# Output projection in four parts with a two-term fold, projections in half passes, and another order of the segment's units

## The chip, the cores and the metric

The kernel runs on one core of a Trainium2 chip. The metric is the device time of one execution in microseconds (us). The unchanged kernel took 1058.44 us (median of 3 runs, 1056.85 to 1059.75). The profiled execution, from which every other time in this part comes, took 1050.84 us; its span from the first to the last instruction is 1049.0 us.

## What is computed

There are two attention branches over the same input and a gate between them. Branch A is a recurrence: 64 segments of 32 rows, and each segment needs the memory that the segment before it produced. Branch B has no such chain over segments of 32; it is work that can be put anywhere.

```python
# A: x (1, 2048, 512); mem (8 rows, 512); Wq, Wk, Wv (512, 32 heads, 128); Wo (32, 128, 512)
for s in range(64):
    h = concat([mem, x[:, 32*s:32*s+32]])                 # 40 rows
    q, k, v = h @ Wq, h @ Wk, h @ Wv                      # per head
    p = softmax(where(mask, q @ k.T * 128**-0.5, -1e9))
    o = sum over heads of (p @ v) @ Wo                    # 40 rows of 512
    mem = o[:, :8]; outs.append(o[:, 8:])                 # a
# B: causal attention in 4 blocks of 512 rows, 32 heads of 16, plus a linear memory; then @ wo   # b
g = sigmoid((x * gate_w).sum(-1, keepdims=True))
return g * a + (1 - g) * b
```

## The kernel before

**Phases.** A first phase loads x and B's weights, transposes x, makes B's projections and stores them in DRAM, while A's weights (four of 4 MB) arrive. From about 86 us on, 64 segments follow (`segment`, called by `plan_a`), each some 14 to 17 us long. A short end follows.

**The recurrence.** `hT[s % 2]` holds a segment's first 32 columns, transposed: 8 of memory and 24 rows of x. These 32 columns are handled alone. The last 8 rows of each segment do not depend on the memory until their queries meet the keys, so the keys, queries and values of the last 8 rows of four segments are projected together, ahead of time, by `left_units`; their output rows are projected together by `ol_units`, a group of four segments later.

**A segment's units.** Each engine executes its own instructions in the order in which they were recorded, and the order of recording is the string `A_ORDER` (line 823), walked once per segment. Its units are:

- `Q0 Q1 K0 K1 V0 V1` (`nat_pass`): a projection pass, 16 heads at a time. `proj` (line 855, matmuls at L862) issues 16 matmuls of 512 columns: four contraction chunks `c` and four column groups `j` of the array, which run side by side. Then comes an eviction of the PSUM bank (`evac`, L319 on ScalarE, L321 on VectorE).
- `TK`, `TQ` (`tr`): 32 x 32 block transposes on VectorE (L868).
- `S` (`scores`, L1006 to L1013, and the exponential at L1019), `M` (`sums`, L1036, then a logarithm L1040 and exponential L1043 which give the reciprocal), `N` (`norm`, L1047 for the main and L1051 for the left part, both on VectorE).
- `PV` (`pv`, L1061 and L1070), and `E0a` to `E1b`: the evictions of its four banks in two halves to `OT_sb`.
- `W0`, `W1` (`wo`, through `out_rows`, matmul at L899): the output projection. For each of 32 heads, each of the four column groups `j` computes its own 128 output columns of that head, so there are 128 matmuls of 128 columns with 128 weight loads. The result (32 rows in each of the four groups) is evicted by ScalarE to `aW_sb`.
- `WT` (`w_t`): one VectorE transpose writes the memory columns of the next segment's `hT`, and GpSimd copies the 24 output rows on to `aT_st`.
- Fillers: `Fc` takes the next `left_units` or `ol_units` pass, `Ff` the next light unit (a gating tail: `brow` at L949, `atr` at L964), `bS` and `bP` a score and a value block of B (L706 with its exponential L714, and L753), `bT` a late piece of B. In three segments of four the two `Fc` are left passes; in the fourth (segments 3, 7, 11 ...) they are the two halves of the previous group's output rows, 64 matmuls each.

`A_ENG` (line 826) says which engine makes each eviction. PSUM has eight banks of 512 f32 columns; `Banks` hands them out while the program is recorded, so a matmul that reuses a bank waits for the eviction that emptied it, whichever unit that belongs to. GpSimd's operations each wait for the one before.

Of the kernel before, what the change touches and what calls it, by code (L numbers as in the profile page):

```python
# [223 lines left out]
def build(nc, es, A_x, A_mem0, A_Wq, A_Wk, A_Wv, A_Wo, B_wq, B_wk, B_wv, B_wo, B_beta, gate_w, out, dbg=None):  # L224
    v = NS()
# [30 lines left out]
    def alloc(stack, *specs):  # L256
        for name, shape, dt, n in specs:
# [3 lines left out]
    alloc(es, ("ident", [128, 128], BF16, 0), ("xT", [128, C, S], BF16, 0), ("hT", [128, C, 128], BF16, 2),  # L261
# [9 lines left out]
          ("aTg", [128, C, 128], BF16, 0))  # L271
# [13 lines left out]
          ("OT_sb", [128, H, L], BF16, 0), ("OTL", [128, H, SEG], BF16, 2), ("aW_sb", [128, 128], BF16, 0), ("aO_sb", [128, 128], BF16, 0),  # L285
# [16 lines left out]
    def Rs(name):  # L302
        if name not in R:
            R[name] = Res(name)
            if name.startswith(("P0", "P1", "Pn", "R0", "R1", "OT", "aW", "aO", "t1", "aTx", "aTl")):
                R[name].readers = list(v.stores)
        return R[name]
# [60 lines left out]
def plan_const(v):  # L368
# [28 lines left out]
    def late():  # L397
        rob, rmk = Rs("onesb"), Rs("mneg")
        gp(lambda g: g.memset(onesb[:], 0.0), rob, "onesb0", True)
        gp(lambda g: g.memset(mneg[:], 0.0), rmk, "mneg0", True)  # L400
        for j in range(4):
# [88 lines left out]
def plan_gates(v):  # L490
# [27 lines left out]
    v.evac("dve", v.hT[0][:, :, 0:v.M], v.pb16[bk][:, 0:C * v.M].rearrange("p (c t) -> p c t", t=v.M), [bk], [Rs("hTm0")], "memT0")  # L518
# [119 lines left out]
class BAttn:  # L638
# [167 lines left out]
    def finish(self, sb, f):  # L806
# [3 lines left out]
        def ft(pe):  # L810
            ins = None
            for q in range(4):
# [11 lines left out]
    Q1 K0 Q0 K1 V0 TK0 TQ0 S0 bP bP TQ1 TK1 bS V1 M0 S1 N0 Fc M1 PV0 E0a N1 E0b Fc PV1 E1b E1a W0 W1 WT bS bT Ff Ff Ff  # L824
    bS bP bS""".split()
A_ENG = dict(K0="act", K1="act", Q0="act", Q1="dve", V0="act", V1="dve", KL0="dve", KL1="dve", QL0="dve", QL1="dve", VL0="dve",
             VL1="dve", OL="act", W="act", E0a="act", E0b="act", E1a="act", E1b="act", last=0)


def plan_a(v, nseg):  # L830
# [10 lines left out]
    OT_sb, OTL, aW_sb, aO_sb, t1_sb, aT_st, g_sb, omg_sb, out2d, g_out = (  # L841
        v.OT_sb, v.OTL, v.aW_sb, v.aO_sb, v.t1_sb, v.aT_st, v.g_sb, v.omg_sb, v.out2d, v.g_out)
# [12 lines left out]
    def proj(bk, lhs, w_sb, b, split, reads, name):  # L855

        def f(pe):
            ins = None
            for c in range(C):
# [33 lines left out]
    def out_rows(bk, b, lhs, reads, name):  # L893

        def f(pe):
            ins = None
            for h in range(16 * b, 16 * (b + 1)):
                for j in range(4):
                    ins = pe.matmul(pb[bk][SEG * j:SEG * (j + 1), 0:128], lhs(h), cols(Wo_sb[:, h, :], j), start=(h == 0), stop=(h == H - 1))  # L899
            return ins  # L900
        P.op("pe", f, reads=reads + [Rs("Wo")], writes=[rbank[bk]], name=name)

    def ol_units(g):
# [5 lines left out]
        for b in range(2):  # L909
            def u(b=b):  # L910
                if b == 0:
                    st["bk"] = B.take(long=True)
                bk = st["bk"]
                out_rows(bk, b, lambda h: OTL[par][:, h, :], [Rs("OTL%d" % par)], "ol%d_%d" % (g, b))
                if b == 1:
                    evac(ENG["OL"], aO_sb[:, :], pb[bk][:, 0:128], [bk], [Rs("aO")], "olev%d" % g)
                    B.give(bk)
            units.append(("c", u))

        def ut():  # L920
            flip(aT_st[par][:, :, :].rearrange("p c (r t) -> p c r t", t=SEG)[:, :, :, SEG - 8:SEG],
                 aO_sb[:, :].rearrange("p (c r i) -> p c r i", c=C, i=8), [Rs("aO")], [Rs("aTl%d" % par)], "aTl%d" % g)
# [55 lines left out]
    def segment(s, fill):  # L978
# [3 lines left out]
        rx = [Rs("hTx%d" % (s % 2)), Rs("hTm%d" % (s % 2))]  # L982

        def nat_pass(m, b, eng):
            w_sb, wr, nat = {"K": (Wk_sb, "Wk", KN_sb), "Q": (Wq_sb, "Wq", QN_sb), "V": (Wv_sb, "Wv", V_sb)}[m]
            bk = B.take()
            proj(bk, lhs, w_sb, b, m != "V", rx + [Rs(wr)], "%s%d_%d" % (m, s, b))
# [11 lines left out]
        def scores(b):  # L999
            bk = sbk[b] = B.take()  # L1000

            def f_sc(pe):
# [8 lines left out]
                for i in range(4):  # L1011
# [6 lines left out]
                 writes=[rbank[bk]], name="sc%d_%d" % (s, b))  # L1018
# [205 lines left out]
```

## Time and profile before

| of the profiled execution | |
|---|---|
| span | 1049.0 us |
| TensorE matmuls busy | 910.7 us (87%) in 30127 |
| weight loads | 562.9 us (54%) in 30149 |
| VectorE busy | 558.5 us (53%) |
| ScalarE busy | 585.8 us (56%) |
| GpSimd busy | 228.1 us (22%) |
| granted TensorE clock | 0.974 |
| segment 30, the third of its four (first projection matmul at 536.6 us, the next segment's at 550.9) | 14.3 us |
| segment 31, the fourth of its four (550.9 to 568.0) | 17.1 us |

The page's groups of instructions name a line, an engine, an operation, its tiles and shape, then the count, the busy time, the mean duration of one in ns, and the idle time of the engine just before them with what ended it. "issue" as the end of an idle time means that the engine waited for nothing that the profile shows. The chain of waits follows the program back from its last instruction, at each step to what released it. The row for DMA queue q8 counts the blocks of instructions themselves that were fetched while the program ran.

### The profile page before, as it was taken

The numbers are of one execution on the slowest core, as the hardware profiler recorded it, in microseconds if no ns is written. First come the engines' busy times: TensorE is split into PE (matmuls) and PEld (weight loads), VectorE is DVE, ScalarE is ACT, GpSimd is POOL, SyncE is SP. The second block draws the span as 40 slices with busy tenths as digits, with TensorE's granted clock in tenths as the row PEclk, the third lists the DMA queues.
The fourth block names the chain that finished last, engine by engine and source line by source line (L and its number), as shares of the span: only waits on it lengthen the run. The fifth ranks groups of instructions, "written<-read, shape, count | busy, mean of one in ns | idle before, by whom it ended". The sixth has DMA issues, their size and how long they took to land.

```text
span 1049.0 us, 65298 instructions
## 1 busy us (share of the span) xinstructions
PE 910.7 (87%) x30127; PEld 562.9 (54%) x30149; DVE 558.5 (53%) x1198; ACT 585.8 (56%) x1211; POOL 228.1 (22%) x603
## 2 busy tenths in 40 slices
PE   7967999789898989899898989989898889988786
PEld 4434565555555555555555555655556555555555
DVE  4665545454454646455465646545564655546433
ACT  4442665565565655655565556655665665554434
POOL 6100221122221222222222222222222222211010
PEclk9997999999999999999999999999999999999989
DMA  9896000000101110010001101000111101000110
GB/s 310 271 373 187 12 12 17 13 21 12 26 15 29 46 37 23 15 25 20 21 16 50 40 15 35 20 23 14 24 46 27 28 20 37 14 14 4 40 33 10
DMA packets 65929, 52.23 MB, mean 50 GB/s; under 512 B 34288, under 2 KB 64120, under 8 KB 64120
## 3 DMA queue, kind: packets, MB, share of 16 engines
q1 hardware_dynamic: 65656, 48.06, 15.6%
q8 instruction: 236, 3.87, 1.5%
q14 instruction: 37, 0.30, 0.1%
HBM read 33.47 MB, written 14.57 MB: 46 GB/s over the span
## 4 chain that ended last, share of the span: by engine, by line
PE 73%; issue 9%; ACT 8%; DVE 6%; DMA 3%; POOL 0%; SPq 0%; ACTq 0%; POOLq 0%; DVEq 0%
PE ps L862 33%; PE ps L899 17%; PE ps L706 5%; ACT PT L714 4%; PE ps L753 4%; PE ps L582 2%; PE ps L557 2%; DVE LN_sb L321 2%; PE ps L1061 2%; ACT R_sb L1043 2%; ACT R_sb L1040 2%; DVE Pn_sb L1047 2%; PE ps L949 1%; DMA Wo_sb<-in_A_Wo_dram 1%; DVE VL L321 1%
## 5 line engine op out<-in xcount | busy, mean ns | idle before, releaser
L899 PE MATMUL ps<-Wo_sb,OT_sb 128*32 128x128 bf16 x8192 | 150.8, 228 | 58.2 <-issue 54.3
L714 ACT ACTIVATE PT<-ps 128x1024 bf16<-128x1024 f32 x160 | 160.1, 1023 | 25.5 <-PE ps L706 21.2
L899 PEld LDWEIGHTS ps<-Wo_sb,OT_sb 128*32 128x32 bf16 x8192 | 126.3, 101 | 72.9 <-issue 62.2
L722 POOL TENSOR_SCALAR_AFFINE_SELECT PT<-PT 128x256 bf16<-128x256 bf16 (+1 forms) x224 | 98.4, 439 | 268.3 <-ACT PT L714 261.0
L862 PE MATMUL ps<-Wq_sb,hT 128*32 128x512 bf16 x2048 | 139.3, 388 | 2.5 <-DVE hT L868 1.9
L868 DVE STREAM_TRANSPOSE hT<-aW_sb 128x128 bf16<-128x128 bf16 x64 | 19.9, 311 | 222.1 <-ACT aW_sb L319 222.1
L862 PE MATMUL ps<-Wk_sb,hT 128*32 128x512 bf16 x2048 | 137.6, 385 | 0.3 <-issue 0.3
L862 PE MATMUL ps<-Wv_sb,hT 128*32 128x512 bf16 x2048 | 134.4, 380 | 0.8 <-ACT V_sb L319 0.8
L319 ACT ACTIVATE KN_sb<-ps 128x512 bf16<-128x512 f32 x128 | 76.4, 597 | 101.1 <-PE ps L862 79.1
L319 ACT ACTIVATE OT_sb<-ps 128x320 bf16<-128x320 f32 x256 | 96.9, 430 | 54.2 <-PE ps L1070 53.2
L868 DVE STREAM_TRANSPOSE KT_sb<-KN_sb 128x512 bf16<-128x512 bf16 x128 | 88.3, 690 | 45.6 <-ACT KN_sb L319 45.3
L319 ACT ACTIVATE aW_sb<-ps 128x128 bf16<-128x128 f32 x64 | 17.8, 278 | 153.8 <-PE ps L899 150.3
L868 DVE STREAM_TRANSPOSE QT_sb<-QN_sb 128x512 bf16<-128x512 bf16 x128 | 83.5, 690 | 10.5 <-ACT QN_sb L319 9.8
L862 PEld LDWEIGHTS ps<-Wk_sb,hT 128*32 128x32 bf16 x2048 | 57.6, 99 | 57.6 <-issue 4.8
L1129 POOL COPY OTL<-OT_sb 128x256 bf16<-128x256 bf16 x64 | 25.4, 397 | 289.8 <-ACT OT_sb L319 289.8
L321 DVE CAST V_sb<-ps 128x512 bf16<-128x512 f32 x64 | 44.3, 692 | 74.7 <-PE ps L862 74.7
L862 PEld LDWEIGHTS ps<-Wq_sb,hT 128*32 128x32 bf16 x2048 | 51.5, 98 | 58.9 <-issue 11.6
L862 PEld LDWEIGHTS ps<-Wv_sb,hT 128*32 128x32 bf16 x2048 | 50.5, 96 | 54.1 <-ACT P_sb L1019 9.8
L321 DVE CAST QN_sb<-ps 128x512 bf16<-128x512 f32 x64 | 43.9, 685 | 39.4 <-PE ps L862 39.1
L706 PE MATMUL ps<-QTj,KTj 32*128 32x384 bf16 (+3 forms) x512 | 63.7, 307 | 0.0
L1047 DVE TENSOR_TENSOR Pn_sb<-P_sb,R_sb 128x160 bf16<-128x160 bf16 x128 | 42.5, 332 | 30.0 <-ACT R_sb L1043 20.7
L1040 ACT ACTIVATE R_sb<-ps 128x160 f32<-128x160 f32 x128 | 38.9, 304 | 34.8 <-PE ps L1036 34.5
(117 smaller groups left out, 1412.5 us busy)
## 6 DMA issues: line engine op xcount, KB each, us to landing
Wk_sb<-in_A_Wk_dram SPq DMA_DIRECT2D x4, 1024.0 KB, 5.9
Wq_sb<-in_A_Wq_dram SPq DMA_DIRECT2D x4, 1024.0 KB, 7.3
Wv_sb<-in_A_Wv_dram SPq DMA_DIRECT2D x4, 1024.0 KB, 9.2
Wo_sb<-in_A_Wo_dram SPq DMA_DIRECT2D x4, 1024.0 KB, 10.7
scr_vd<-V SPq DMA_DIRECT2D x16, 136.0 KB, 6.0
Vj<-scr_vd SPq DMA_DIRECT2D x32, 68.0 KB, 2.4
Wo_sb<-in_A_x_dram SPq DMA_DIRECT2D x4, 512.0 KB, 7.5
scr_kTd<-stgk SPq DMA_DIRECT2D x16, 128.0 KB, 7.1
```

The lines of the kernel that those rows point to most:

```text
L319: P.op("act", lambda a: a.activation(dst, src, ACT.Copy), reads=[v.rbank[k] for k in bks], writes=dres, name=name)
L321: P.op("dve", lambda d: d.tensor_copy(dst, src), reads=[v.rbank[k] for k in bks], writes=dres, name=name)
L706: ins = pe.matmul(v.pb[bks[x]][:, o:o + w], KT[e][r, 128 * kc:128 * (kc + 1)], QT[r, q0:q0 + w], start=True, stop=True, tile_position=(r.s ...
L714: P.op("act", lambda a: a.activation(pt[:, :, :], v.ps[:, bks[0]:bks[1] + 1, :], ACT.Exp, scale=v.SCALE_B), reads=[v.rbank[b] for b in bks ...
L722: P.op("gp", lambda g, mv=mv: g.affine_select(mv, mv, [[0, mv.shape[1]], [1, 128]], ALU.is_ge, 0.0, base=0, channel_multiplier=-1), reads= ...
L753: ins = pe.matmul(v.pb[ob][:, o:o + 17], pt[:, x, col:col + 128], V[:, kc, 17 * h:17 * (h + 1)], start=first, stop=True, skip_group_check= ...
L862: ins = pe.matmul(pb[bk][SEG * j:SEG * (j + 1), :], lhs(c), cols(w, j) if split else w[:, 512 * j:512 * (j + 1)], start=(c == 0), stop=(c ...
L868: P.op("dve", lambda d: d.transpose(dst, src), reads=reads, writes=writes, name=name)
L899: ins = pe.matmul(pb[bk][SEG * j:SEG * (j + 1), 0:128], lhs(h), cols(Wo_sb[:, h, :], j), start=(h == 0), stop=(h == H - 1))
L1040: P.op("act", lambda a: a.activation(R_sb[:, b, :], pb[bk][:, 224:384], ACT.Ln), reads=[rbank[bk]], writes=[Rs("R%d" % b)], name="ln%d_%d" ...
L1047: P.op("dve", lambda d: d.tensor_tensor(wide(Pn_sb, b)[:, :, 0:L], wide(P_sb, b)[:, :, 0:L], R_sb[:, b, :].rearrange("p (i q) -> p i q", q ...
L1129: P.op("gp", lambda gq: gq.tensor_copy(OTL[par][:, :, 8 * r:8 * r + 8], OT_sb[:, :, SEG:L]), reads=[Rs("OT%d_%d" % (c, hf)) for c in range ...
```

## The change

**Output projection.** `out_rows` becomes `out_part`. Column group `j` now takes heads 4k + j instead of a quarter of the columns, and a matmul covers 256 output columns in one of two banks (`hf`), so there are 64 matmuls of 256 columns. Each group then holds a partial sum over 8 heads, and the four must be added. `part_hi` (ScalarE) copies the partial sums to bf16 (`WH`), `part_lo` (VectorE) stores what that rounding lost (`WL`), and `fold` multiplies both by a 0/1 matrix, which adds the four groups and transposes the result at once: 8 matmuls of 32 columns. The memory goes from there straight to the next `hT`, the other rows straight to `aT_st`, all on VectorE. The transpose on VectorE and GpSimd's copy are gone. `ol_units` is changed in the same way, with `LN_sb` as its buffer.

**Half passes.** `hT`'s memory columns are now two pieces of dependence (`hTm0_0`, `hTm0_1`), and each projection pass is two units, `x` (chunks 0, 1) and `y` (chunks 2, 3), so that a pass may begin when half of the memory is there. Evictions, exponentials and reciprocals are units of their own (`k q v X L n H l`).

**Order and engines.** A new `A_ORDER` and `A_ENG`: the left passes' evictions go from VectorE to ScalarE, `E0a` goes from ScalarE to VectorE, the left part of the normalisation from VectorE to GpSimd, and late pieces of B (`bT`) come in the middle of the output projection instead of after it.

```diff
 A_ORDER = """
-    Q1 K0 Q0 K1 V0 TK0 TQ0 S0 bP bP TQ1 TK1 bS V1 M0 S1 N0 Fc M1 PV0 E0a N1 E0b Fc PV1 E1b E1a W0 W1 WT bS bT Ff Ff Ff
-    bS bP bS""".split()
-A_ENG = dict(K0="act", K1="act", Q0="act", Q1="dve", V0="act", V1="dve", KL0="dve", KL1="dve", QL0="dve", QL1="dve", VL0="dve",
-             VL1="dve", OL="act", W="act", E0a="act", E0b="act", E1a="act", E1b="act", last=0)
+    Q1x Q1y K0x K0y Q0x Q0y k0 K1x K1y V0x q0 q1 V0y k1 TK0 TQ0 v0 S0 TQ1 bP X0 bS V1x TK1 V1y M0 L0 v1
+    S1 N0 X1 Fc M1 L1 n0 n1 PV0 E0a E0b N1 Fc bP PV1 W0a E1b W0b E1a bT W1b W1a H0 H1 bP l0 l1 bS
+    Ff F0 F1 hm0 hm1 Ff bS ax Ff""".split()
+A_ENG = dict(K0="act", K1="act", Q0="act", Q1="dve", V0="act", V1="dve", KL0="act", KL1="act", QL0="act", QL1="act", VL0="act", VL1="act", OL="act", ax="dve", hm="dve", n="gp", E0a="dve", E0b="act", E1a="act", E1b="act", last=0)
...
-            for c in range(C):
+            for c in cs:
...
-    def out_rows(bk, b, lhs, reads, name):
+    def out_part(bks, hf, ks, first, lhs, reads, name):
 
         def f(pe):
             ins = None
-            for h in range(16 * b, 16 * (b + 1)):
+            for k in ks:
                 for j in range(4):
-                    ins = pe.matmul(pb[bk][SEG * j:SEG * (j + 1), 0:128], lhs(h), cols(Wo_sb[:, h, :], j), start=(h == 0), stop=(h == H - 1))
+                    ins = pe.matmul(pb[bks[hf]][SEG * j:SEG * (j + 1), 0:HD], lhs(4 * k + j), Wo_sb[:, 4 * k + j, HD * hf:HD * (hf + 1)],
+                                    start=(first and k == ks[0]), stop=False, skip_group_check=True)
             return ins
...
+    def part_hi(bks, hf, hi, res, name):
+        c = slice(HD * hf, HD * (hf + 1))
+        P.op("act", lambda a: a.activation(hi[:, c], pb[bks[hf]][:, 0:HD], ACT.Copy), reads=[rbank[bks[hf]]],
+             writes=[Rs(res[0][hf])], name="%sh%d" % (name, hf))
+
+    def part_lo(bks, hf, hi, lo, res, name):
+        c = slice(HD * hf, HD * (hf + 1))
+        P.op("dve", lambda d: d.tensor_tensor(lo[:, c], pb[bks[hf]][:, 0:HD], hi[:, c], ALU.subtract),
+             reads=[rbank[bks[hf]], Rs(res[0][hf])], writes=[Rs(res[1][hf])], name="%sl%d" % (name, hf))
+        B.give(bks[hf])
+
+    def fold(bks, hf, hi, lo, res, name):
...
+            for n in range(2):
+                for m, t in enumerate((hi, lo)):
+                    ins = pe.matmul(pb[bks[hf]][:, SEG * n:SEG * (n + 1)], t[:, 256 * hf + 128 * n:256 * hf + 128 * (n + 1)], v.fold[:, :],
+                                    start=(m == 0), stop=(m == 1))
...
-        rx = [Rs("hTx%d" % (s % 2)), Rs("hTm%d" % (s % 2))]
+        rx = lambda half: [Rs("hTx%d" % (s % 2)), Rs("hTm%d_%d" % (s % 2, half))]
...
-            P.op("dve", lambda d: d.tensor_tensor(left(Pn_sb), left(P_sb), grp04(R_sb[:, b, :]), ALU.mult),
+            P.op(ENG["n"], lambda d: d.tensor_tensor(left(Pn_sb), left(P_sb), grp04(R_sb[:, b, :]), ALU.mult),
...
-        def w_t():
-
-            nxt = (s + 1) % 2
-            rm = Rs("hTm%d" % nxt)
-            quads = hT[nxt][:, :, :].rearrange("p c (k z) -> p c k z", z=SEG)
-            flip(quads[:, :, :, 0:M], aW_sb[:, :].rearrange("p (c k t) -> p c k t", c=C, t=M), [Rs("aW")], [rm], "hm%d" % (s + 1))
-            P.op("gp", lambda gq: gq.tensor_copy(
-                aT_st[par][:, :, SEG * r:SEG * (r + 1) - M].rearrange("p c (k t) -> p c k t", t=M), quads[:, :, 1:4, 0:M]),
-                 reads=[rm], writes=[Rs("aTx%d_%d" % (par, r))], name="atx%d" % s)
+        def w_fold(hf):
+            if hf == 0:
+                wb["f"] = B.pair()
+            fold(wb["f"], hf, v.WH, v.WL, w_res, "wf%d" % s)
+
+        def w_mem(hf):
+            evac(ENG["hm"], hT[nxt][:, 2 * hf:2 * hf + 2, 0:M], folded(wb["f"])[:, hf, :, 0:M], [wb["f"][hf]], [Rs("hTm%d_%d" % (nxt, hf))],
+                 "hm%d_%d" % (s + 1, hf))
...
```

## The prediction

> **What bounds the kernel now.** I read the page's busy times first, then the costliest groups, then the waits, then the chain of waits over single segments. From the page:
>
> ```profile
> PE 910.7 (87%) x30127; PEld 562.9 (54%) x30149; DVE 558.5 (53%) x1198; ACT 585.8 (56%) x1211; POOL 228.1 (22%) x603
> q8 instruction: 236, 3.87, 1.5%
> PE 73%; issue 9%; ACT 8%; DVE 6%; DMA 3%; POOL 0%; SPq 0%; ACTq 0%; POOLq 0%; DVEq 0%
> L899 PE MATMUL ps<-Wo_sb,OT_sb 128*32 128x128 bf16 x8192 | 150.8, 228 | 58.2 <-issue 54.3
> ```
>
> TensorE bounds it. The other engines are half idle, so work moved to them is free unless TensorE waits for it. The last line is the point: the output projection is busy for 150.8 us and idle for 58.2 us more, with no releaser. The waits view says how often:
>
> ```profile
> PE ps L899 <- issue: 66.2, 54, 2.3
> PEld ps L1061 <- ACT OT_sb L319: 24.9, 50, 1.0
> ```
>
> The first line, with the smaller "issue" rows of L1061 and L1070, comes to some 78 us. The chain over segment 29, which has no such stall, and over 31, which has the previous group's output rows as its two fillers, shows where they fall:
>
> ```profile
> 523.49 4.43 PE ps L862 x80
> ...
> 532.11 1.05 PE ps L862 x16
> 533.16 0.27 PE ps L1061 x14
> 533.43 0.10 PE ps L1070 x15
> 533.52 2.09 PE ps L899 x128
> 535.61 0.32 PE ps L706 x4
> ```
>
> ```profile
> 561.10 1.14 issue
> 562.24 0.22 PE ps L1061 x6
> 562.46 0.10 PE ps L1070 x15
> 562.55 1.72 PE ps L899 x105
> 564.28 1.45 issue
> 565.73 0.52 PE ps L899 x23
> ```
>
> The projections issue 80 matmuls in 4.43 us, the output projection 128 in 2.09 us. Stalls come only in or beside the second kind. The q8 row gives the cause: 3.87 MB in 236 blocks is 16.4 KB each, and 60276 matmuls and weight loads over 236 are 255 per block. So one block holds about 256 instructions. In the trace two fetches never start less than 3.25 us apart (median 3.93). 128 output matmuls with their loads are one block, used up in 2.09 us. TensorE then stands about 1.2 us.
>
> [...] a pass is four rounds of four side by side and takes 0.86 us, or 215 ns a round. [...] 2.09 us over 32 rounds is 65 ns, [...] the trace's 256-element sum on GpSimd takes 733 ns.
>
> **The change part by part.** Stage times before are differences of the start times of matmul groups in the trace, averaged over the first three segments of each four, then the fourth.
>
> | stage | three of four | fourth |
> |---|---|---|
> | projections, to S0 | 4.5 | 4.45 |
> | S0 to S1 | 2.2 | 2.15 |
> | S1 to PV0 | 1.4 | 1.7 |
> | PV0 to PV1 | 1.8 | 2.3 |
> | PV1 to W | 0.3 | 0.85 |
> | W | 2.95 | 4.0 |
> | W to next segment | 1.3 | 1.1 |
> | sum | 14.45 | 16.6 |
>
> *Half passes and projections.* The same matmuls in the same time: 4.5 stays. The halves help only if the second half of the memory comes late, and below it does not.
>
> *S0 to S1.* One bP (0.25 us) leaves for later, and the wait of V1 for the exponential (0.2 us in segment 29) goes with the bank: −0.2.
>
> *W itself.* 128 matmuls of 128 columns become 64 of 256. By the 512-column rows a round of four takes 107 ns, so 16 rounds take 1.72 us instead of 2.09. Half as many instructions over nearly the same time is 13 ns each against 8. Counted along the new order, 256 instructions from Fc or PV0 on take 3.4 to 3.7 us, hardly below a fetch. I take 0.1 us of stall left where 0.9 was (2.95 less 2.06). The late piece of B now inside costs 0.15 us on average. W goes from 2.95 to 1.97: −1.0.
>
> *PV0 to PV1.* E0a moves to VectorE. Between rows of 424 ns for 256 elements and 690 for 512 it takes 0.49 us. It stands there behind the left pass's transpose (0.71), which waits for that pass's eviction on ScalarE (0.60), and N1 stands behind it. With the first pass at T = 0: left pass ends 7.6, evicted 8.4, transposed 9.15, E0a to 9.55, N1 to 9.85, PV1 at 9.9. PV0 is at 7.7. That is 2.2 us against 1.8: +0.4. The left part of the normalisation on GpSimd [...] From 0.22 to 0.73 it stays inside the wait for N1 or adds under 0.1.
>
> *W to the next segment.* Before: eviction 0.28, transpose 0.31, about 0.85 from W to a new first pass, filled with bS, bP, bS. After: the first half's last matmul ends 0.21 before W. Then 0.18 to ScalarE, high part 0.37 (between 346 for 224 and 430 for 320), low part 0.42 (the 424 row), four fold matmuls 0.13, 0.18 to VectorE, memory copy 0.17 (the 32-element copy). The second half follows 0.38 later. TensorE has bP 0.25 and bS 0.33, waits 0.3 for the first fold, folds 0.13, waits 0.25, folds 0.13, bS 0.33: 1.7 us, so +0.85. Where a gating tail falls (16 segments) its 1.08 us fill those waits, which gives back 0.1 on average; bT leaves, −0.15; its VectorE chain of 1.8 us (219 + 176 + 424 + 174 + 253 + 274 + 424 ns, in 24 segments) stands ahead of the low part and delays it by 0.45, +0.15. Net +0.75. Who waits: both folds, then the next segment's first pass, which is the recurrence.
>
> *Fourth segments.* The two fillers shrink to 32 matmuls of 256 columns each. PV0 now waits for a bank from the second logarithm: S1 to PV0 2.0, +0.3. PV0 to PV1: 1.45, since no left pass stands ahead of E0a: −0.85. The output-row evictions share one buffer, so high, low, high, low go one after another, and W's second half waits for that bank: PV1 to W 0.4 (−0.45), W 1.72 + 0.65 + 0.15 = 2.5 (−1.5). The end costs +0.7. With S0 to S1, −2.0 in all.
>
> *At nothing.* ScalarE gains 6 left evictions of 0.6 per group and loses E0a; [...] both stay under 75% busy. The constant for the fold is made in the first phase under the weight loads.
>
> **Sum.** 48 × (−0.2 + 0.4 − 1.0 + 0.75 = −0.05) = −2; 16 × −2.0 = −32. 1058.4 − 34 = 1025.
>
> **The rivals.**
>
> *All waits are covered.* If fillers or shorter latencies cover what I add between PV0 and PV1 and at the end, only the stalls count: −0.8 × 48 and −2.4 × 16 = −77, or 981. For it: 87% busy leaves little else on the path. Against: the new order has only bP and bS between W and the fold.
>
> *The chain takes back more than the stalls gave (slower).* Each segment now passes ScalarE, VectorE, TensorE and VectorE instead of ScalarE and VectorE. If this and E0a's place cost 0.7 us more than I count in three of four and the fourth gains 1.0, it is +34 − 16, or 1076. For it: bT's chain ahead of the low part, and bank reuse tied to evictions now on ScalarE. Against: durations are measured ones, and no engine is near full.
>
> *Fetching stays the limit.* If 256 instructions still take less than a fetch in the dense stretch, 0.4 us a segment come back: +26 on the forecast, 1051.
>
> **How the numbers follow.** Forecast 0.5, all covered 0.22, slower 0.16, fetch-limited 0.12. The forecast's own terms carry ±0.4 us in three of four and ±0.7 in the fourth, ±22 together. The low end of 986 leaves out half of the covered case; the high end of 1060 takes in the fetch-limited one and leaves out most of the slower one. Faster by over 0.3%: 0.76; within 0.3% (1055 to 1062): 0.07; slower: 0.17.
>
> **What would show it.** The matmul groups of the output projection should number about 4096 with the idle time ending in "issue" down from 54 us to under 15, and q8 should carry about 201 blocks (235 less 8960 instructions over 256). W should take 1.7 us. The fold's matmuls should show idle time of about 0.5 us a segment released by VectorE's low part. PV1 should wait for N1. Fourth segments should be near 14.7 us, no longer the longest by 2. I am wrong if the fold's waits are covered, if stalls stay at L899, or if the fourth segments wait for PSUM banks longer than I count.

## The result and the profile after

The changed kernel takes 1027.11 us (median of 4 runs, 1022.69 to 1032.21), the kernel before 1059.1 us beside it. The ratio is 0.968, with a 95% interval of 0.9597 to 0.9762. A second measurement, against other runs of the kernel before, gave 0.9702 (0.9661 to 0.9744). Medians and ratios are of fast executions; one of the four of the kernel with the dense padding below, at 1131 us, was in a slower state and is left out. The prediction was 1025 us, so the total and its sign hold. The terms of the sum hold less well, and part of the total came through the granted clock (0.974 in the trace of before, 0.982 in that of after), which no term had.

The lines of the page after that answer to those shown of before:

```profile
PE 937.6 (91%) x25669; PEld 561.7 (55%) x25669; DVE 584.2 (57%) x1374; ACT 656.2 (64%) x1355; POOL 259.1 (25%) x672
...
q8 instruction: 202, 3.31, 1.4%
...
PE 29%; ACT 3%; DVE 2%; issue 1%; ACTq 0%; DVEq 0%
...
L908 PE MATMUL ps<-Wo_sb,OT_sb 128*32 128x256 bf16 x4096 | 141.0, 282 | 13.2 <-DVE LN_sb L920 8.3
```

The output projection has 4096 matmuls instead of 8192, its idle time has fallen from 58.2 us to 13.2, and what ends that is no longer "issue" but VectorE. 34 blocks of instructions fewer were fetched. The shares of the chain can't be set against those of before: they add up to 35% only, since the chain could not be followed further back. What TensorE waits for must be read from the waits view instead (columns: engine, tile and line waiting, who releases it, total us, times, longest us):

```profile
PEld ps L930 <- ACT WH L915: 23.9, 39, 1.2
...
PE ps L930 <- DVE WL L920: 15.3, 41, 0.9
...
PEld ps L867 <- ACT PT L719: 9.1, 29, 0.9
...
PE ps L908 <- DVE LN_sb L920: 8.3, 16, 0.8
...
PEld ps L908 <- issue: 2.3, 7, 0.6
```

The stalls at the output projection are gone (last line; 76.4 us in 58 times on the weight loads before). In their place stand the fold (L930), which waits first for the high part and then for the low part, the next first pass (L867), which waits for a PSUM bank that an exponential of B still reads, and in the fourth segments W, which waits for the low part of the output rows. The two L930 rows overlap: loads and matmuls of the same fold wait in the same stretch.

From the first segment on, all stretches over 60 ns in which TensorE neither multiplies nor loads weights add up to 116.8 us before and 62.9 after. Those longer than 0.3 us that end 1.15 to 1.55 us after the end of a fetch of instructions, which I count as fetch stalls, were 78 us and are 12.

The stalls cost more than their own length. In the traces of before and after the granted TensorE clock is 1.00 or 0.50 wherever it is recorded, and a stretch of one value that lies whole within the trace lasts 3.41 us or a multiple of it (in before, 0.50 from 505.95 to 509.36 us). Between the starts of segments 1 and 61 the kernel before has 8 half-clock stretches, 30.7 us together; the changed kernel has one of 3.4 us. In the 3.41 us ahead of each of the 8, TensorE stood idle for 1.57 to 1.89 us; ahead of the one after, for 1.49. Over all windows of that length in before, the mean is 0.40 us, and one in twenty reaches 1.5. So in these two kernels the half clock follows where stalls pile up. That does not account for every case: with the four parts alone (below) two of seven such stretches begin after only 0.9 us of idle time. All this is read from the traces; no experiment was made for it. Segment 50 of after shows the price: its projections, with one stretch of 3.41 us in them, take 6.01 us in place of 4.33, half of 3.41 more. At that price the half clock makes up to 14 us of the gain (an estimate from these lengths).

The stage times, by the method of the prediction (differences of starts; W ends with the modelled end of its last matmul). The first segments and the last three are left out. Each cell has three of four, then the fourth; the middle rows belong to experiments below.

| kernel | to S0 | S0–S1 | S1–PV0 | PV0–PV1 | PV1–W | W | W–next | sum |
|---|---|---|---|---|---|---|---|---|
| before | 4.51 / 4.45 | 2.17 / 2.15 | 1.43 / 1.72 | 1.79 / 2.30 | 0.30 / 0.84 | 2.96 / 4.02 | 1.33 / 1.12 | 14.48 / 16.61 |
| new order alone | 4.65 / 4.36 | 1.97 / 1.95 | 1.42 / 1.72 | 2.05 / 2.68 | 0.32 / 0.81 | 3.23 / 4.17 | 1.22 / 1.10 | 14.86 / 16.80 |
| parts alone | 4.47 / 4.66 | 2.15 / 2.15 | 1.44 / 1.90 | 1.76 / 1.35 | 0.46 / 0.83 | 2.16 / 2.63 | 2.70 / 2.60 | 15.12 / 16.11 |
| parts alone, B's piece last | 4.57 / 4.50 | 2.15 / 2.15 | 1.43 / 1.91 | 1.76 / 1.35 | 0.38 / 0.82 | 2.20 / 2.67 | 2.27 / 3.12 | 14.77 / 16.52 |
| after | 4.37 / 4.33 | 1.97 / 1.95 | 1.43 / 1.97 | 2.03 / 1.60 | 0.33 / 0.38 | 2.22 / 3.03 | 1.88 / 2.11 | 14.22 / 15.38 |

W gives back 0.74 us in three of four, and the stage behind it takes 0.55. The end of segment 28, the first of its four, in the timeline of after (start, duration, engine, line, operation, tiles, count, idle time before it and who ended it):

```profile
506.29 1.93 PE L908 MATMUL ps<-Wo_sb,OT_sb 128*32 128x256 bf16 x64
...
508.12 0.66 ACT L915 ACTIVATE WH<-ps 128x256 bf16<-128x256 f32 x2 [0.85 <-PE ps L908]
...
508.54 0.76 DVE L920 TENSOR_TENSOR WL<-ps,WH 128x256 bf16<-128x256 f32 x2 [1.54 <-PE ps L758]
...
509.11 0.18 PE L930 MATMUL ps<-fold,WH 128*128 128x32 bf16 x1 [0.27 <-DVE WL L920]
...
509.39 0.17 DVE L322 CAST hT<-ps 128x16 bf16<-128x16 f32 x1
...
510.01 0.55 PEld L867 LDWEIGHTS ps<-Wq_sb,hT 128*32 128x32 bf16 x16 [0.30 <-ACT PT L719]
```

64 matmuls end at 508.2, bP and bS fill TensorE until 508.84, and from there it waits 0.27 us for the first low part. The memory columns are there at 509.56 and 509.90; the first pass begins at 510.01, after a wait that is put down to B's exponential (PT), 1.8 us after W.

The other half of the result lies in the fourth segments. Timeline of after in segment 31, where the output rows of the group before meet W (the columns are the same):

```profile
547.95 0.38 ACT L915 ACTIVATE LN_sb<-ps 128x256 bf16<-128x256 f32 x1
...
548.36 0.42 DVE L920 TENSOR_TENSOR LN_sb<-ps,LN_sb 128x256 bf16<-128x256 f32 x1
...
548.87 0.38 ACT L915 ACTIVATE LN_sb<-ps 128x256 bf16<-128x256 f32 x1 [0.54 <-PE ps L1126]
549.15 0.76 ACT L320 ACTIVATE OT_sb<-ps 128x320 bf16<-128x320 f32 x2
...
549.83 0.26 PEld L908 LDWEIGHTS ps<-Wo_sb,OT_sb 128*32 128x32 bf16 x11 [0.78 <-ACT OT_sb L320]
549.86 1.09 PE L908 MATMUL ps<-Wo_sb,OT_sb 128*32 128x256 bf16 x24 [0.52 <-DVE LN_sb L920]
```

The second high part (548.87) starts only when the first low part has ended (548.78), since both column halves share one name for their buffer. The two evictions of `OT_sb`, which W needs, stand behind it on ScalarE, and the second low part, which frees the bank that W writes to, ends at 549.71. TensorE stands for half a microsecond. The matmul that ends the wait, the ninth of W, is the first that writes to the second bank, and it starts 0.15 us after that low part has ended.

### The profile page after: what moved, and what is told of

Its sections match the earlier page's. It is cut to its first block, busy times and chain, and to the rows that moved or that the text cites. A ratio compares the mean times of both kernels' runs of the same rounds, so it can differ in the third digit from the quotient of the medians.

```text
span 1027.3 us, 57156 instructions
## 1 busy us (share of the span) xinstructions
PE 937.6 (91%) x25669; PEld 561.7 (55%) x25669; DVE 584.2 (57%) x1374; ACT 656.2 (64%) x1355; POOL 259.1 (25%) x672
## 5 line engine op out<-in xcount | busy, mean ns | idle before, releaser
L908 PE MATMUL ps<-Wo_sb,OT_sb 128*32 128x256 bf16 x4096 | 141.0, 282 | 13.2 <-DVE LN_sb L920 8.3
L867 PE MATMUL ps<-Wq_sb,hT 128*32 128x512 bf16 x2048 | 134.5, 382 | 2.2 <-ACT PT L719 1.3
L867 PE MATMUL ps<-Wk_sb,hT 128*32 128x512 bf16 x2048 | 133.8, 381 | 0.0
L867 PE MATMUL ps<-Wv_sb,hT 128*32 128x512 bf16 x2048 | 133.6, 380 | 0.0
L908 PEld LDWEIGHTS ps<-Wo_sb,OT_sb 128*32 128x32 bf16 x4096 | 101.8, 99 | 28.9 <-ACT OT_sb L320 11.9
L915 ACT ACTIVATE WH<-ps 128x256 bf16<-128x256 f32 x128 | 42.4, 381 | 91.5 <-PE ps L908 87.8
L920 DVE TENSOR_TENSOR WL<-ps,WH 128x256 bf16<-128x256 f32 x128 | 48.4, 419 | 67.5 <-ACT WH L915 32.8
L867 PEld LDWEIGHTS ps<-Wk_sb,hT 128*32 128x32 bf16 x2048 | 55.9, 97 | 55.5 <-DVE aTg L1009 1.9
L320 ACT ACTIVATE OT_sb<-ps 128x320 bf16<-128x320 f32 x192 | 76.0, 431 | 15.8 <-PE ps L1126 14.6
L867 PEld LDWEIGHTS ps<-Wq_sb,hT 128*32 128x32 bf16 x2048 | 50.0, 97 | 57.6 <-ACT PT L719 9.1
L1107 POOL TENSOR_TENSOR Pn_sb<-P_sb,R_sb 128x64 bf16<-128x64 bf16 x128 | 45.9, 359 | 137.5 <-ACT R_sb L1097 121.8
L867 PEld LDWEIGHTS ps<-Wv_sb,hT 128*32 128x32 bf16 x2048 | 49.7, 96 | 53.5 <-issue 12.4
L758 PEld LDWEIGHTS ps<-Vj,PT 128*128 128x128 bf16 x1280 | 42.6, 96 | 32.3 <-issue 31.1
L758 PE MATMUL ps<-Vj,PT 128*128 128x17 bf16 x1280 | 57.6, 172 | 0.0
```

The source lines that it names most:

```text
L320: P.op("act", lambda a: a.activation(dst, src, ACT.Copy), reads=[v.rbank[k] for k in bks], writes=dres, name=name)
L758: ins = pe.matmul(v.pb[ob][:, o:o + 17], pt[:, x, col:col + 128], V[:, kc, 17 * h:17 * (h + 1)], start=first, stop=True, skip_group_check= ...
L867: ins = pe.matmul(pb[bk][SEG * j:SEG * (j + 1), :], lhs(c), cols(w, j) if split else w[:, 512 * j:512 * (j + 1)], start=(c == 0), stop=(c ...
L908: ins = pe.matmul(pb[bks[hf]][SEG * j:SEG * (j + 1), 0:HD], lhs(4 * k + j), Wo_sb[:, 4 * k + j, HD * hf:HD * (hf + 1)], start=(first and k ...
L915: P.op("act", lambda a: a.activation(hi[:, c], pb[bks[hf]][:, 0:HD], ACT.Copy), reads=[rbank[bks[hf]]], writes=[Rs(res[0][hf])], name="%sh ...
L920: P.op("dve", lambda d: d.tensor_tensor(lo[:, c], pb[bks[hf]][:, 0:HD], hi[:, c], ALU.subtract), reads=[rbank[bks[hf]], Rs(res[0][hf])], w ...
```

## The experiments

**The two halves of the change, each alone.** First the new order and engines, with the output projection, transpose and GpSimd copy of before:

```diff
-                for j in range(4):   # out_part: 64 matmuls of 256 columns in two banks
-                    ins = pe.matmul(pb[bks[hf]][...], lhs(4 * k + j), Wo_sb[:, 4 * k + j, HD * hf:HD * (hf + 1)], ...)
+                for j in range(4):   # 128 matmuls of 128 columns in one bank
+                    ins = pe.matmul(pb[bk][...], OT_sb[:, h, 0:SEG], cols(Wo_sb[:, h, :], j), ...)
...
-    ... W1b W1a H0 H1 bP l0 l1 bS Ff F0 F1 hm0 hm1 Ff bS ax Ff
+    ... W1b W1a H0 bP hm ax bS Ff Ff bS Ff
```

> The new order and engines with the old output projection: 128 matmuls of 128 columns per segment, split at the same four places, then the old eviction, VectorE transpose and GpSimd copy, no fold; the output rows also in the old form. If instruction fetching is what the four parts cured, the stalls come back at the output projection: idle time ending in issue of 45 us or more on it, 236 instruction blocks, and a time of 1040 to 1055 us, most of the gain gone although the fold's 0.85 us per segment at the end is saved. If the order brought the gain and the four parts are a mere detail, it stays at 1027 or, without the fold's waits, goes below 1015 us.

It took 1074.09 us: 1.0075 of before (1.0044 to 1.0106). That is above the 1040 to 1055 expected: the order alone gains nothing. Its waits view, where L1155 is the output projection:

```profile
PE ps L1155 <- issue: 54.6, 44, 2.2
```

The fetch stalls are all there: 80.5 us by the count above. The table shows what the order does by itself: S0 to S1 −0.20, PV0 to PV1 +0.26, as in the changed kernel. The hoped-for shortening of the rest does not appear while W keeps its stalls (W is even 0.27 longer, and 0.28 longer where the clock was full in both). The granted clock was 0.958 against 0.974, with 15 half-clock stretches against 8 between segments 1 and 61; the 0.14 us more in the projections come with them.

Then the four parts and the fold, in the order and with the engines of before:

```diff
-    S1 N0 X1 Fc M1 L1 n0 n1 PV0 E0a E0b N1 Fc bP PV1 W0a E1b W0b E1a bT W1b W1a H0 H1 bP l0 l1 bS
-    Ff F0 F1 hm0 hm1 Ff bS ax Ff
+    ... N0 n0 Fc M1 L1 PV0 E0a N1 n1 E0b Fc PV1 E1b E1a W0a W0b W1b W1a H0 H1 l0 l1 bS bT F0 F1 hm0 hm1
+    ax Ff Ff Ff bS bP bS
```

> The output projection in four parts with its fold, but in the old order of units and on the old engines (left evictions, all normalisation and both E0 where they were); the fold stands after the first score block and late piece of B. By the fetch theory the parts carry the gain: 1022 to 1038 us, with 202 blocks and little idle time ending in issue at the output projection, and about 0.3 us per segment more at the end than with the new order, which puts a value block and a score block ahead of the fold. If the order carried the gain, it is at 1050 us or above.

It took 1081.32 us: 1.0134 (1.0094 to 1.0174). This one was missed by 43 us and more: the gain is not the sum of what the halves give alone. The waits view of this kernel:

```profile
PEld ps L930 <- ACT WH L915: 36.6, 64, 1.1
...
PE ps L867 <- DVE hT L322: 15.8, 14, 1.7
```

The fetch stalls are gone here too (13.5 us), and W is 2.16. But the stage behind W has doubled, from 1.33 to 2.70: every fold waits, and in 14 segments the first pass waits up to 1.7 us for the memory copy. In this mapping the late piece of B (`bT`) is recorded before the copies, and its chain on VectorE comes first. A second mapping takes that away:

```diff
-    ... H0 H1 l0 l1 bS bT F0 F1 hm0 hm1 ax Ff Ff Ff bS bP bS
+    ... H0 H1 l0 l1 bS bP F0 F1 hm0 hm1 bT Ff Ff Ff bS ax
```

> The four parts with the fold, set again in the order and with the engines of the kernel before, but with the late piece of B recorded after both memory copies and with the two other fillers between the low parts and the folds, so that VectorE's chain of 1.8 us for that piece is no longer ahead of the memory. If the loss of the earlier mapping (1081 us) was only this misplacement, the stage from W to the next segment falls from 2.6 to 2.9 us to the 1.9 us of the changed kernel, and the time to 1081 - 0.8 x 64 = 1030 us. If the fold's chain needs the new order's other moves (first half's banks first, engines freed ahead of it), it stays at 2.2 us or more and the time is 1050 us or longer.

It took 1070.17 us: 1.005 (1.0026 to 1.0073). That is the second branch of the expectation: the stage behind W is 2.27 and not 1.9, so the misplacement was not all. From its waits view:

```profile
PEld ps L930 <- ACT WH L915: 25.6, 63, 1.1
...
PE ps L711 <- DVE amem L807: 18.7, 13, 1.8
```

The fold's wait is now near that of the changed kernel (25.6 us against 23.9), so it is not what separates the two. New is a wait for `amem`, the end of `bT`'s chain: `bT` gives its PSUM bank free only then, and the score block behind it needs that bank. Without those 18.7 us it would be near 0.987 of before (an estimate, 1.005 less 18.7 of 1066 us), still no 0.97. Two mappings do not exhaust the old order, so what the best one would give stays open. What is shown: neither half alone made the kernel faster, and of the three orders tried the parts pay only in the one that hides the fold and B's late piece.

**Is it the fetch of instructions?** The same 64 needless matmuls of 16 columns were put into the changed kernel twice: once into the middle of W, once between two projection passes, where the matmuls are long.

```diff
+            ins = pe.matmul(pb[bk][SEG * j:SEG * (j + 1), 256:272], v.ident[...], v.ident[:, 0:16], ...)   # x64
...
-    ... E1a bT W1b W1a ...
+    ... E1a D bT W1b W1a ...      # dense
...
-    Q1x Q1y K0x K0y Q0x ...
+    Q1x Q1y K0x K0y Z Q0x ...     # sparse
```

> The changed kernel with 64 needless matmuls of 16 columns and their weight loads per segment, put in the middle of the output projection; their results are never read. By their own time (16 such take 0.13 us in the left scores of the kernel before) 64 take 0.52 us, 33 us in all. By the fetch theory 256 instructions then pass in about 2.6 us, less than the 3.25 us that a fetch takes, and each segment also stalls some 0.5 to 0.7 us: 1027 + 33 + 30 to 45 = 1090 to 1105 us, 236 blocks, idle time ending in issue of over 25 us at the output projection. If there is no fetch limit, only their own time counts: about 1060 us, like the next kernel.

> The changed kernel with the same 64 needless matmuls, put between two projection passes instead, where 32 matmuls and loads take 0.86 us; their results are never read. Both theories say that they cost their own time and little else: 1027 + 33 = 1060 us, at most 1067, with as many blocks (236) as the kernel that has them in the output projection. The difference between the two is the test: 0 if fetching does not matter, 30 us or more if it does.

Dense: 1114.45 us, 1.0426 (1.0335 to 1.0516), above the 1090 to 1105 expected. Sparse: 1070.89 us, 1.0063 (1.0029 to 1.0097). The instructions and the blocks are the same (234 in both), and the place is worth 44 us. The expectations had 30 us or more. From the waits view of the dense one, where L1162 is the added matmul:

```profile
PE ps L1162 <- issue: 16.7, 19, 2.5
PE ps L908 <- issue: 13.7, 13, 1.9
```

and of the sparse one, where it is L1164:

```profile
PE ps L1164 <- issue: 2.4, 2, 1.2
```

Fetch stalls by the count above are 51.8 us in the dense kernel and 7.5 in the sparse one; W grows by 1.18 us (2.22 to 3.40) where the projections grow by 0.61 (4.37 to 4.98). So the stall is brought back by instructions alone, and only where they are used up quickly. That settles the cause of the stalls that the change removed. The half clock goes the same way (9 stretches between segments 1 and 61 in the dense kernel, 4 in the sparse one), so some of the 44 us is its share. The average pace does not show the stalls: in before a block was needed only every 4.4 us (1049 us over 236), and fetches started as little as 3.25 us apart, yet the stalls counted there come to 78 us. How many blocks are held ahead of their use was not shown.

**Is the fold's low part on the path?** The changed kernel as it is, as zero, and one in which the segments' fold takes the high part only.

```diff
-            fold(wb["f"], hf, v.WH, v.WL, w_res, "wf%d" % s)
+            fold1(wb["f"], hf, "wf%d" % s)            # hi only: 2 matmuls a half instead of 4
...
-            units["l%d" % b] = lambda b=b: part_lo(...)
+            units["l%d" % b] = lambda b=b: B.give(wb["bks"][b])
```

> The changed kernel itself, on the same chip as the next three and against the same runs of the kernel before: the ratio of the first measurement, 0.96 to 0.976. It is the zero from which the next three are read.

> The changed kernel without the low part in the segments' fold: four fold matmuls instead of eight, which wait for ScalarE's copy alone; the rounding of the partial sums to bf16 is then not made good in the segment's own rows and memory. As predicted, the low part (0.42 us) lies on the chain to the next segment's first pass, and taking it out saves 0.3 to 0.4 us in each segment: 18 to 26 us, ratio 0.018 to 0.025 under the changed kernel's. The rival: the next segment's first pass in most segments waits longer for its PSUM bank, which the exponential of the score block ahead of the fold holds until about 1.9 us after the output projection; then only the fold's own matmuls are saved, at most 8 us (0.007).

1028.1 us and 1017.6 us: 0.9702 and 0.9592 (0.9551 to 0.9634). The gain is 10.5 us, far less than the low part's 0.42 us in each of 64 segments (27 us). W to the next segment goes from 1.89 to 1.73 only. The waits view of the kernel without the low part says what took its place:

```profile
PEld ps L867 <- ACT PT L719: 27.3, 33, 1.0
```

9.1 us of this in the changed kernel, 27.3 here: the first pass waits for the bank under B's exponential as soon as the fold no longer holds it up. Two waits end nearly together, and taking one away shows the other.

**That bank.** So the first pass was given the spare bank in place of the shared ones:

```diff
-                bank[m, b] = B.take()
+                bank[m, b] = B.take(long=(m == "Q" and b == 1))
```

> The changed kernel with the first projection pass of a segment in a bank of the two kept for long uses, so that it no longer reuses the bank of the score block ahead of the fold. If that bank is what holds the next segment's first pass, 0.2 to 0.3 us go in some 35 to 45 segments: 7 to 13 us, ratio 0.007 to 0.012 under the changed kernel's, and the waits of the first pass for the exponential of B vanish. If the low part alone sets the end of the segment, nothing changes (within 0.003).

1028.81 us, 0.9704 (0.9661 to 0.9748): no change, where 7 to 13 us were expected if the bank held the pass. From its waits view:

```profile
PEld ps L867 <- ACT KN_sb L320: 23.1, 61, 0.4
...
PEld ps L867 <- ACT V_sb L320: 13.8, 58, 0.5
```

The stage behind W does fall by 0.1, to 1.78, and the wait for the exponential is gone from the first pass. Weight loads of later passes now wait for the evictions of earlier ones, and the stage to S0 grows by 0.06 (4.33 to 4.39 where the clock was full). PV1 to W grows by 0.05. The banks are handed out in another order; which exchange makes which wait was not traced. A bank wait moved, it was not removed.

**A version put together from these readings.** It adds to that bank a second left pass in the spare bank, the left transposes behind N1, the last quarters of W by column half, a score block between the two folds, and names of their own for the buffers of the output rows:

```diff
-    ... PV0 E0a E0b N1 Fc bP PV1 W0a E1b W0b E1a bT W1b W1a H0 H1 bP l0 l1 bS Ff F0 F1 hm0 hm1 Ff bS ax Ff
+    ... PV0 E0a E0b N1 LT Fc LT bP PV1 W0a E1b W0b E1a bT W1b0 W1a0 W1b1 W1a1 H0 H1 bP l0 l1 bS
+    Ff F0 bA F1 hm0 hm1 Ff bS ax Ff
...
-    o_res = (("LN0", "LN0"), ("LN1", "LN1"))
+    o_res = (("LN0", "LN0r"), ("LN1", "LN1r"))
```

> The changed kernel with the waits found so far taken away together: the first pass and the second left pass in the spare long bank; the left passes' transposes recorded after the second normalisation on VectorE, so that E0a and N1 no longer stand behind the first of them; the last two quarters of the output projection by column half, so that the first fold's chain starts 0.21 us earlier; a score block between the two folds (not in fourth segments); the two halves of the output rows' evictions no longer tied to each other. By my stage sums 0.3 to 0.35 us between PV0 and PV1, 0.3 to 0.45 at the end of the segment, and 0.5 us more in the fourth segments: 40 to 58 us less than the changed kernel, 970 to 990 us, ratio 0.917 to 0.933. If TensorE's own work were the limit already (91% busy), 10 us or less.

1020.93 us, 0.9629 (0.9587 to 0.9672): 7 us for six edits, where 40 to 58 were expected. The left transposes behind N1 did take 0.13 us from PV0 to PV1 (2.03 to 1.90), and fourth segments fell by 0.45 us, but the projections grew (4.33 to 4.41 at full clock) with the same waits of weight loads as above (23.5 us at KN_sb). The gain might come from the fourth segments alone, so the next runs took single edits.

**Single edits.** Half passes that begin together:

```diff
-        rx = lambda half: [Rs("hTx%d" % (s % 2)), Rs("hTm%d_%d" % (s % 2, half))]
+        rx = lambda half: [Rs("hTx%d" % (s % 2)), Rs("hTm%d_0" % (s % 2)), Rs("hTm%d_1" % (s % 2))]
```

> The changed kernel with one edit: each half pass waits for both halves of the memory, so the halves begin together. The recorded forecast costs half passes at nothing: within 0.3% of the changed kernel (1025 to 1031 us). If the half that begins early is what covers the second fold's chain (the second memory copy ends about 0.4 us after the first), up to 0.35 us in each of 64 segments come back: 1050 us.

1029.68 us, 0.9661 (0.9612 to 0.9711). As expected, nothing clear of the noise is lost: the stage behind W is 1.94 against 1.88, where the forecast counted nothing.

The names of the output rows' buffers (the left passes that use the same buffer got the second name too; not shown):

```diff
-    o_res = (("LN0", "LN0"), ("LN1", "LN1"))
+    o_res = (("LN0", "LN0r"), ("LN1", "LN1r"))
```

> The changed kernel with one edit: in the previous group's output rows the high part and the low part are made with a dependence of their own for each column half, so the order is high, high, low, low with each low part waiting for its own high part only, not high, low, high, low one after another over one shared buffer name. The forecast's step says the fourth segments' W waits 0.65 us for the bank from this; in the trace of the changed kernel W waits for the low part 0.52 us in each of 16 fourth segments. If that serial chain is the wait, fourth segments' W falls from 3.03 to about 2.5 us and the time by 8 us (0.992 of the changed kernel). If W waits for ScalarE's queue rather than for the chain, nothing moves.

1021.39 us, 0.9593 (0.9546 to 0.964), as expected: 8.3 us less than the run above on the same chip, and 6 to 7 less than the two measurements of the changed kernel. Timeline of this kernel, the same place as in the fourth segment shown of after:

```profile
550.08 0.94 PE L908 MATMUL ps<-Wo_sb,OT_sb 128*32 128x256 bf16 x18
551.27 0.61 PE L908 MATMUL ps<-Wo_sb,OT_sb 128*32 128x256 bf16 x14 [0.24 <-issue]
```

Most of the half microsecond is gone, and the rows of the waits view that put W behind `LN_sb` and `OT_sb` shrink from 8.3 and 11.9 us to 0.4 and 0.6. W in fourth segments falls from 3.03 to 2.58, the whole by 0.36 us. This edit is one of the six, and it alone gives all that they gave together.

Two waits are left in W of fourth segments. The ninth matmul still starts 0.2 us late in most of them, each time 0.15 us after the end of the second low part, so the bank is still the limit. The pause before 551.27 ends 1.27 us after the end of a fetch, like the stalls counted above; five of the 13 fourth segments averaged here have such a pause of 0.15 to 0.6 us.

The same with B's late piece moved behind the memory copies:

```diff
-    ... W0b E1a bT W1b W1a H0 H1 bP l0 l1 bS Ff F0 F1 hm0 hm1 Ff bS ax Ff
+    ... W0b E1a W1b W1a H0 H1 bP l0 l1 bS Ff F0 F1 hm0 hm1 bT Ff bS ax Ff
```

> The edit of ol_split, and the late piece of B taken out of the middle of the output projection and recorded after the two memory copies. The output projection loses that piece's matmuls (0.3 us in 24 of 64 segments), which then lie in TensorE's wait for the copies, and VectorE's chain of 1.8 us for it no longer stands ahead of the low part (0.45 us in the same segments): 24 x 0.75 = 18 us less, with the 8 us of ol_split 1028 - 26 = 1002 us. If that chain then delays the first evictions of the next segment or of the output rows, and these hold the banks, half of it is given back: about 1012 us. If other waits take its place at once, 1020 us as with ol_split alone.

1056.6 us, 0.9914 (0.9881 to 0.9947): 35 us slower than without the move, where a gain was expected. W falls as it should, to 1.98 and 2.30, but in three of four the stage behind W grows by 0.45 and the projections of the next segment by 0.39 (0.32 where the clock was full). Timeline of this kernel at the end of a segment:

```profile
550.97 0.40 PE L1006 MATMUL ps<-ident,aTg 128*128 128x128 bf16 x4
...
552.73 0.42 DVE L807 TENSOR_TENSOR amem<-ps,rden 128x256 f32<-128x256 f32 x1
...
553.30 0.39 PE L711 MATMUL ps<-QTj,KTj 32*128 32x384 bf16 x4 [1.94 <-DVE amem L807]
```

The memory copies end at 551.16. TensorE nevertheless stands 1.94 us, because the score block ahead of the next first pass takes the bank that `bT` holds until its last VectorE operation reads it. The VectorE chain did leave the low part, and came back as a bank. In the changed kernel this wait is 0.5 us in the whole program: in the middle of W the chain has the rest of W and the fold to hide in. This is what the placement of `bT` in the new order is worth, and I had counted that placement only as a cost.

## Why the prediction was right, and where its steps were not

*The bound and its cause.* Right: 64 short matmuls put back bring the stalls back, in the dense place only. Fetching is hardly the limit any more: 0.3 us of "issue" at L908's matmuls and 2.3 us at its loads, against "under 15"; 202 blocks against about 201. By the count of fetches above 12 us of stalls are left.

*What stalls cost.* The prediction counted a stall at its own length. That the half clock behind stalls would go too was in no term; the projections, on which 12.3 of the 30.7 us of before fall, were put at no change.

*W.* −1.0 forecast, −0.74 measured. The rate was right: in the trace of after, rounds of four matmuls start 109 ns apart (107 forecast). But the 2.09 us of before contain the modelled end of the last matmul, which outlasts its round, and the 1.72 us do not; measured in the same way, W's matmuls take 1.93 us, 0.19 more than 16 rounds. For that reason, and for a few slower rounds, the prediction's 65 ns a round at 128 columns is misread: most rounds of before start 56 ns apart, and at 512 columns 216. B's late piece costs 0.24 us on average in three of four (2.22 less 1.98 in the run without it), not 0.15. The other 0.05 is stall or less, against 0.1 forecast.

*W to the next segment.* +0.75 forecast, +0.55 measured. The chain was read rightly: high part 0.381, low part 0.419, wait for the first fold 0.27 against 0.3, and 1.79 us in segment 28 against 1.7. What fails is the +0.15 for B's late piece ahead of the low part (whose seven VectorE times add up to 1.94 us, not 1.8): the segments of the three with that piece and no gating tail have 1.65 us behind W, those without either have 1.77. What the sum did not have is the bank under B's exponential, which ends at nearly the same moment; with the low part gone it holds the first pass. TensorE's matmuls waited less for the low part than the half microsecond a segment that was named as a sign: 15.3 us, 0.24 a segment.

*PV0 to PV1.* +0.4 forecast, +0.24 measured; the new order alone shows +0.26, so it is the order's cost. That it comes through E0a and N1, as argued, holds for about half: recording the left transposes behind N1 took 0.13 away. TensorE's idle time in this stage did not grow (0.38 us before, 0.29 after). Its busy time did, from 1.41 to 1.74, since a value block of B (`bP`) was moved in. In segment 28 that block and N1 end within 0.04 us of each other, and only 7 waits in the whole program (5.0 us) are put down to N1. E0a took 0.474 us against 0.49.

*GpSimd's left part.* The median is 309 ns and the mean 359, because about a third took some 440. That lies between the bounds of 0.22 us, which VectorE took for it in before, and 0.73, the 256-element sum on GpSimd. In the waits view of after TensorE waits for it once, 0.4 us in the whole program.

*S0 to S1, projections, half passes.* −0.20 as forecast. The projections gave 0.14 more than the nothing that was forecast. Without the segments whose passes meet a half-clock stretch (mainly three of before, with 5.7 to 6.2 us for the usual 4.33, and one of after), 0.08 is left. Half passes at nothing: right.

*Fourth segments.* −2.0 forecast, −1.23 measured, and this is the step that failed most. S1 to PV0 (+0.25 for +0.3) and PV1 to W (−0.46 for −0.45) are near, PV0 to PV1 gave less (−0.70 for −0.85), and the end costs more (+0.99 for +0.7). W was forecast at 2.5 and is 3.03. The serial chain through one buffer name was seen, with 0.65 us: in the trace the ninth matmul starts 0.7 us late, and of this the second name removes about 0.5. Too small were the matmuls, again by the modelled end (1.93 for 1.72), and B's piece (0.28 for 0.15: 2.58 less 2.30). The run without that piece and with the second name still has 2.30, 0.37 more than the matmuls: about 0.17 is what is left of the wait for the low part, 0.14 is fetch stalls in four of 13 segments, and the rest is spread. Why the end costs 0.29 more than forecast I have not settled. The fourth segments are 15.38 us, not near 14.7, and 1.16 longer than the others.

*The sum.* Three of four gave 0.26 us each instead of 0.05, the fourth 1.23 instead of 2.0: 48 × 0.26 + 16 × 1.23 = 32 us where 34 were forecast. That the total is so close is luck. Two errors of 10 and 12 us cancel. And a third of the 32 us came with the clock: without the stages that meet a half-clock stretch, three of four go from 14.33 to 14.19 us and the fourth from 16.25 to 15.38, which is 21 us. The other executions agree: those of before beside the experiments had a granted clock of 0.96 on average, those of the changed kernel 0.98. The two traces as wholes lie only 21.7 us apart (1049.0 and 1027.3), since the first phase and the first and last segments gain nothing, and since the profiled execution of before, at 1050.84 us, was faster than its median.

*The rivals.* "All waits are covered" was wrong: the fold waits in about 40 of 64 segments. "Fetching stays the limit" was wrong. "The chain takes back more" was not what happened, but the four parts in the order of before come near it: 1.0134 and 1.005. The sign hung on the order more than 0.16 says, and the prediction did not ask what each half would do alone.

## What to carry to other kernels

Where the busiest engine has idle time with no releaser next to short instructions, count instructions per microsecond against the distance between fetches (here 256 instructions, and 3.25 us at the least): fewer and longer instructions are then worth more than their own time (here fetch stalls went from 78 us to 12), but work that leaves the engine for a chain over others must be given something to hide behind in the same change. Look at the granted clock behind the stalls as well (here 30.7 us of half clock became 3.4), and compare stage times at the same clock. When buffers or banks are handed out in the order of recording, a piece moved off one queue can hold its bank for longer (here a score block waited 1.94 us for the one of `bT`), so ask of every move what is released later; and look whether two halves of a buffer share one name before looking for cleverer orders, since here that name alone was worth as much as six edits together, itself among them.

## What was not expected of the hardware

64 matmuls of 16 columns with their loads cost about 0.6 us a segment between long matmuls and 1.2 us among short ones (4.37 to 4.98, 2.22 to 3.40). Idle time of 1.57 us or more within 3.41 us stood ahead of every half-clock stretch of the kernel before from segment 1 to 61. And a round of four matmuls in four column groups starts 56 ns after the one before at 128 columns, 109 at 256 and 216 at 512; dividing a whole stretch by its rounds gives more (65 at 128), because the modelled end of the last matmul and a few slower rounds are in it.
